# Attention and MLP on one core: query rows of the middle chunk in a tile of their own, small copies on ScalarE, and a second h phase issued ahead over eight banks

## The chip, the core and the metric

The kernel runs on one core of one Trainium2 chip. The metric is the device time of a launch in microseconds (us). A core has TensorE (PE; its weight loads are shown apart as PEld), VectorE (DVE), ScalarE (ACT), GpSimd (POOL) and SyncE (SP). Each runs its own instruction list and waits for the others by semaphores. The kernel's matmuls write to eight PSUM banks of 512 float32 columns.

## What is computed

Eight batches, eight heads of width 64, 512 local and 32 global tokens. Global queries see all 544 keys; a local query sees the 32 global keys and the local keys at most 32 positions away. The result, 4352 tokens of 512 features, goes through an MLP with a quick GELU.

```python
s_g = scale * q_g @ [k_g, k_l].T            # softmax over 544 keys
s_ll = where(|i - j| <= 32, scale * q_l @ k_l.T, -1e9)
s_l = [scale * q_l @ k_g.T, s_ll]           # softmax over 32 + 512 keys
attn = concat(sm(s_g) @ [v_g, v_l], sm(s_l) @ [v_g, v_l])
x = attn as (8*544, 512)
h = x @ w_in                                # 512 -> 2048
out = (h * sigmoid(1.702 * h)) @ w_out      # 2048 -> 512
```

## The kernel before

**Quads.** A batch's eight heads are two quads of four heads, side by side in four groups of 32 partitions. `nq[b]` holds the two quads of batch b; they are called `a` (first) and `c` (second). The 64 features of a token are kept as 32 pairs of bf16, one pair in four bytes, so that one 4-byte 32x32 transpose on VectorE (`Tk` for keys, `Tq` for queries) turns a whole quad. A local token is 16 r + t: its query lies in the tile `qt` at row t + 4, place r (`qt` is 24 rows of 32 four-byte places; rows 0 to 3 and 20 to 23 are filled up with global queries). A matmul takes one half of each pair (`e` is 0 or 1) and so reads every second bf16.

**Attention of a quad of the class `Wide` (batches 2 to 7, 12 quads).** `Tk` and `Tq` turn keys and queries; `ext` (line 530) adds the global queries to `qt` by three VectorE copies (lines 536 to 538) and the global keys to `kT` by a fourth (540). `S(0)` and `S(1)` (line 542) are the scores of two rounds of three parts each, by the table `PARTS` (line 510): six sets of four matmuls per round, one per head, side by side. The middle chunk (c = 2: keys 192 to 319, query places 10 to 21) is part of both rounds: 10 rows of 12 places in round 0, 9 rows of 12 in round 1. Both read `qt[:, row, 10:22]`, 48 bytes out of each row's 128. `X` is the exponential on ScalarE, `M` the mask on VectorE, `U` and `Gm` (lines 569 and 583) the products with values, and `RXG` the normalisation on VectorE, which writes `xL`, the MLP's input.

**Phases.** The order of the work on every engine is the order in which the code issues it (`tc.manual_schedule()`). The h phase of batch i is 16 steps `h_step(i, fc)` (line 617): four matmuls of 512 columns into a PSUM bank (606), tanh on ScalarE (613, tile `th`, two buffers), and a multiply-add on VectorE (614) that writes `gT` and frees the bank. The banks `hp` come from the pool `psP`, which has four; the other four are two pairs of banks, `psS`, given out by `spair()` for the scores. The o phase of batch i (`phase_o`, line 837) is four tiles of 16 matmuls (631), and between them the attention of the next quads: `c` of batch i + 1, then `a` of batch i + 2.

**Around the change.** Batches 0 and 1 use the class `Quad` and an order written out by hand. In batch 0's o phase (lines 769 to 811) the attention of batch 1 is made; `nq[2][0].Tq()` and `transpose_g(4, 6, "k")` (lines 794 and 795) stand behind `a.R()`. Then comes batch 1's h phase (lines 816 to 835): two steps' matmuls issued ahead (818), `G()` of batch 1's second quad behind step 1, `a.Tk()` behind step 2, the turning of global queries and `a.ext()` behind step 7, `a.S(0)` and `a.X(0)` behind step 10, and `a.M(0)` at the end. `phase_o(1)` then begins with `c.T()` and `c.ext()` (849 and 850) on VectorE, and PE does `a.S(1)`, `o(0)`, `c.S(0)`. In later batches `a2.T()` and `a2.ext()` (862 to 864) and `a2.S(0)` lie in the o phase before, and the h phase holds nothing but the 16 steps (890 to 892). `k32` and `q32` (134 and 135) are float32 tiles for the first load, `th4` (737) holds four tanh results of batch 0's h phase.

Of the kernel before, what the change touches and what calls it, by code (L numbers as in the profile page):

```python
# [12 lines left out]
F32 = mybir.dt.float32  # L13
BF16 = mybir.dt.bfloat16
# [6 lines left out]
def kernel(  # L21
# [91 lines left out]
    def load_g(lo, hi, names="kqv"):  # L113
        for name, dst, src in (("k", rkg, kgf), ("q", rqg, qgf)):
            if name in names:
                nc.gpsimd.dma_start(out=dst[:, lo:hi, :], in_=src[:, lo:hi, :])
        if "v" in names:
            load_turned(nc.gpsimd, rvg[:, lo:hi, :D], vgf[:, lo:hi, :])
# [12 lines left out]

    load(0, kq=False)
    rk, rq = loaded[0]
    k32 = ld.tile([128, 16 * D], F32, name="k32", bufs=1)
    q32 = ld.tile([128, 16 * D], F32, name="q32", bufs=1)
    halves = (slice(0, 8 * D), slice(8 * D, 16 * D))
    load_g32("q", qgf)
    for f in halves:
# [95 lines left out]
    def transpose_g(lo, hi, names="qk"):  # L234
        for name, dst, s in (("q", qgT, rqg), ("k", kgT, rkg)):
            if name not in names:
                continue
            nc.vector.transpose(dst[:, lo:hi, :32], s[:, lo:hi].bitcast(F32))
# [37 lines left out]
    def spair():  # L276
        return [psS.tile([128, 2, 512], F32, name="s4", tag="s%d" % i) for i in range(2)]
# [4 lines left out]
    class Quad:  # L282
# [17 lines left out]
        def Tk(self, lo=0, hi=16):  # L300
            if lo == 0:
                self.kT = att.tile([128, Sl], F32, name="kT", bufs=2)
                self.k = self.kT.bitcast(BF16).rearrange("p (m e) -> p m e", e=2)
            nc.vector.transpose(self.kT.rearrange("p (r t) -> p t r", t=16)[:, lo:hi],
                                loaded[self.b][0][:, self.u].bitcast(F32)[:, 32 * lo : 32 * hi])
# [9 lines left out]
        def ext(self, cs=(0, 1, 2, 3)):  # L315
            for c in cs:
                (r0, nr), t0, n = WIN[c], (0, 20, 1, 20)[c], (4, 3, 3, 4)[c]
                nc.vector.tensor_copy(
                    self.qt[:, t0 : t0 + n, r0 : r0 + nr],
                    qgT[:, self.Q, : n * nr].rearrange("p (t r) -> p t r", t=n))  # L320
# [49 lines left out]
        def X(self, rnd, between=None):  # L370
            e = self.E[rnd]
            if len(self.ps) == 4:
                for j in range(4):
                    n = RW + 32 if j == 2 else RW
                    nc.scalar.activation(e[:, j, :n], self.ps[j][:, :n], AF.Exp, scale=scale)
                return
            for i in range(2):
                if i and between:
                    between()
                nc.scalar.activation(e[:, 2 * i : 2 * i + 2, :RW], self.ps[i][:, :, :RW], AF.Exp, scale=scale)  # L380
            if rnd == self.gr:
                nc.scalar.activation(e[:, 2, RW:], bank(self.ps, 2)[:, RW : RW + 32], AF.Exp, scale=scale)
# [136 lines left out]
    OUTER = ((0, 0, 128), (0, 472, 96), (1, 160, 128), (1, 460, 96), (1, 0, 96))  # L519

    class Wide(Quad):
        def Tk(self):
            self.kT = att.tile([128, 4, 320], F32, name="kT", bufs=2)
            flat = self.kT.rearrange("p c s -> p (c s)")
            nc.vector.transpose(flat[:, 0:Sl].rearrange("p (r t) -> p t r", t=16),  # L525
                                loaded[self.b][0][:, self.u].bitcast(F32))
            nc.vector.tensor_copy(self.kT[:, 2:4, 0:96], self.kT[:, 0:2, 96:192])
            self.k = flat.bitcast(BF16).rearrange("p (m e) -> p m e", e=2)

        def ext(self):  # L530
            def g(n, r, m):
                src = qgT[:, self.Q, : n * r].rearrange("p (t o r) -> p t o r", o=1, r=r)
                return src.to_broadcast([128, n, m, r])

            ends = self.qt[:, 0:4, :].rearrange("p t (g r) -> p t g r", r=8)
            nc.vector.tensor_copy(ends[:, :, 0:4:3], g(4, 8, 2))
            nc.vector.tensor_copy(self.qt[:, 20:23, 4:28].rearrange("p t (g r) -> p t g r", r=12), g(3, 12, 2))
            nc.vector.tensor_copy(self.qt[:, 1:4, 10:22],
                                  qgT[:, self.Q, :36].rearrange("p (t r) -> p t r", r=12))
            nc.vector.tensor_copy(self.kT[:, :, 96:128], kgT[:, self.Q : self.Q + 1].to_broadcast([128, 4, 32]))  # L540

        def S(self, rnd):
            self.ps = spair()
            for c, r_, at, lo, hi, _, _, _, r0, nr in PARTS:
                if r_ != rnd:
                    continue
                n = (hi - lo) * nr
                for e in range(2):
                    for j in range(4):
                        p = slice(32 * j, 32 * j + 32)  # L550
                        nc.tensor.matmul(  # L551
                            bank(self.ps, j)[:, at : at + n],
                            lhsT=self.k[p, KEYS[c] : KEYS[c] + 128, e],
                            rhs=self.q[p, lo:hi, r0 : r0 + nr, e],
                            start=(e == 0), stop=(e == 1), skip_group_check=True,
                        )
            self.E[rnd] = att.tile([128, 4, EW], BF16, name="e%d" % rnd)

        def X(self, rnd):
            n = (EW, EW - 12)[rnd]  # L560
            for i in range(2):
                nc.scalar.activation(self.E[rnd][:, 2 * i : 2 * i + 2, :n], self.ps[i][:, :, :n], AF.Exp, scale=scale)  # L562

        def M(self, rnd):
# [39 lines left out]
    def h_mm(i, fc, hp, kcs):  # L604
        for kc in kcs:
            nc.tensor.matmul(hp[:, : width(i)], lhsT=w_in_c[:, fc // 8, kc, fc % 8 // 2, :, fc % 2],  # L606
                             rhs=(xL[i] if i < B else xG)[:, kc, :],
                             start=(kc == 0), stop=(kc == NKC - 1))
# [8 lines left out]
    def h_step(i, fc):  # L617
        if fc == 0:
            gTs[i] = moe.tile([128, FC, TB], BF16, name="gT")
        hp = pbank("hp")  # L620
        h_mm(i, fc, hp, range(NKC))
        h_act(i, fc, hp)
# [111 lines left out]
            h_mm(0, fc, bank(pt, fc), (kc,))  # L734
    a.G()
    c.Gm()
    th4 = th4s[0] = ld.tile([128, 4, TB], F32, name="th4", bufs=1)

    def tanh2(hf):
        f = slice(2 * hf, 2 * hf + 2)  # L740
# [18 lines left out]
    def osteps(i, *sts):  # L759
        for tci, f4 in sts:  # L760
            o_mm(i, 4 * tci + f4)
# [22 lines left out]
    c.S(0)  # L784
    c.X(0)
    c.M(0)
    osteps(0, (2, 2), (2, 3))
    c.S(1)
    a.ekUs(c, 1)
# [1 line left out]
    for unit in range(3):  # L791
        a.U(unit)
    a.R()
    nq[2][0].Tq()
    transpose_g(4, 6, "k")
    c.M(1)
    c.eg()
    pt = spair()
# [14 lines left out]
    load_v(3)  # L813
    load(4)
    load_g(8, NQ, "kq")
    gTs[1] = moe.tile([128, FC, TB], BF16, name="gT")
    hps = [pbank("hp") for _ in range(2)]
    for fc, kcs in ((0, (0, 1)), (1, (0, 1)), (0, (2, 3)), (1, (2, 3))):
        h_mm(1, fc, hps[fc], kcs)
    for fc in range(FC):  # L820
        if fc < 2:
            h_act(1, fc, hps[fc])
        else:
            h_step(1, fc)
        if fc == 1:
            nq[1][1].G()
        if fc == 2:
            a.Tk()
        if fc == 7:
            transpose_g(4, 6, "q")  # L830
            a.ext()
        if fc == 10:
            a.S(0)
            a.X(0)
    a.M(0)

    def phase_o(i):
        b = i + 1
        n = b + 1
        a, c = nq[b]  # L840
        if n < B:
            nq[n] = (Wide(2 * n), Wide(2 * n + 1))
            a2, c2 = nq[n]

        def o(tci):
            for f4 in range(4):
                o_mm(i, 4 * tci + f4)

        c.T()
        c.ext()  # L850
        a.S(1)
        a.X(1)
        a.M(1)
        o(0)
        c.S(0)
        a.UG()
        c.X(0)
        a.RXG()
        c.M(0)
        o(1)  # L860
        if n < B:
            a2.T()
            transpose_g(2 * n, 2 * n + 2)
            a2.ext()
        c.S(1)
        c.X(1)
        c.M(1)
        if n < B:
            o(2)
            a2.S(0)  # L870
            c.UG()
            a2.X(0)
        else:
            for f4 in range(3):
                o_mm(i, 8 + f4)
            for unit in range(3):
                c.U(unit)
            c.Gm(bank(spair(), 0))
            o_mm(i, 11)
        c.RXG()  # L880
        if n < B:
            a2.M(0)
        o(3)
        if i + 3 < B:
            load_v(i + 3)
        if i + 4 < B:
            load(i + 4)

    for i in range(1, B):
        if i > 1:  # L890
            for fc in range(FC):
                h_step(i, fc)
        if i + 1 < B:
            phase_o(i)
    for st in range(FC):
# [35 lines left out]
```

## Time and profile before

| | us |
|---|---|
| Median of 3 runs | 303.5 (302.71 to 303.75) |
| The profiled execution's own time | 303.15 |
| Its span, from first to last instruction | 301.4 |
| PE / DVE / ACT / POOL busy | 292.7 / 218.3 / 167.3 / 75.5 |
| Batch 1's h phase on PE, first to last step | 53.9 to 69.6 |
| First score matmul of batch 2's second quad | 74.89 |
| Batch 2's h phase to the same point | 123.5 to 141.6 |

The profile gives times from the span's start. A group line names the source line, engine, operation, output <- input, shape and count, then the busy time, the mean duration of one in ns, and the idle time of the engine ahead of it with what ended it. A matmul's duration runs from its start to its result, so matmuls overlap: 512-column matmuls last 379 ns and start 216 ns apart. The granted TensorE clock was 1.00 throughout. VectorE and ScalarE instructions also overlap a little; the multiply-adds of line 614 last up to 689 ns and start 604 ns apart when nothing holds them up.

### The profile page before, as it was taken

Reading aid. Unit: us, or ns where it says so; the run is one execution under the profiler, and the core shown is the slowest. Engines: PE = TensorE matmul, PEld = TensorE weight load, DVE = VectorE, ACT = ScalarE, POOL = GpSimd, SP = SyncE. Lnnn points to the kernel's source line nnn. Section 1 sums busy time; section 2 is a strip of 40 time slices with the busy share of each in tenths; the row PEclk is TensorE's granted clock in tenths of the full one; section 3 lists DMA queues with packets and bytes.
Section 4 is the critical chain, followed back from the end, with each engine's and each line's share of the span. In section 5 each row is a group of like instructions: output and inputs, shape, how many; then the busy total and the mean of one; then the engine's idle time right before and its main releaser. Section 6 shows DMA issues by size and latency. Waiting matters only on the chain.

```text
span 301.4 us, 8146 instructions
## 1 busy us (share of the span) xinstructions
PE 292.7 (97%) x3409; PEld 150.1 (50%) x3409; DVE 218.3 (72%) x445; ACT 167.3 (56%) x258; POOL 75.5 (25%) x126
## 2 busy tenths in 40 slices
PE   6899999998999999999999999999999999999995
PEld 6454445443554455445454455445454455446653
DVE  6578857879976887778967887788877866683320
ACT  4838484476537756476446736567447651763421
POOL 8742655972045000900054002600000000000000
PEclk9999999999999999999999999999999999999999
DMA  7999999999459512990269412900220012101122
GB/s 191 178 209 209 206 180 226 123 181 183 66 78 145 100 37 54 124 153 7 70 70 145 86 38 72 124 0 11 63 63 10 0 48 64 35 0 28 44 69 71
DMA packets 59220, 28.35 MB, mean 94 GB/s; under 512 B 47664, under 2 KB 49072, under 8 KB 59184
## 3 DMA queue, kind: packets, MB, share of 16 engines
q0 software_dynamic: 51024, 17.57, 51.9%
q1 hardware_dynamic: 7680, 9.61, 12.0%
q10 hardware_dynamic: 480, 0.66, 0.7%
q8 instruction: 26, 0.43, 0.6%
q14 instruction: 10, 0.08, 0.1%
HBM read 36.31 MB, written 8.91 MB: 150 GB/s over the span
## 4 chain that ended last, share of the span: by engine, by line
PE 84%; DVE 5%; DMA 4%; ACT 4%; issue 1%; SPq 0%; ACTq 0%
PE op L631 35%; PE hp L606 33%; PE ov L577 5%; PE s L551 4%; DVE gT L614 2%; DMA ek<-ek 2%; DMA g32k<-in_k_g_dram 2%; ACT th L613 1%; PE s L606 1%; ACT e L380 1%; PE ov L459 1%; PE op L643 1%; ACT e L562 1%; DVE e L567 1%; DVE kT L525 1%
## 5 line engine op out<-in xcount | busy, mean ns | idle before, releaser
L631 PE MATMUL op<-w_out_sb,gT 128*128 128x512 bf16 x528 | 121.8, 380 | 0.0
L614 DVE SCALAR_TENSOR_TENSOR gT<-th,hp 128x512 bf16<-128x512 f32 (+1 forms) x140 | 91.2, 657 | 41.3 <-ACT th L613 40.2
L606 PE MATMUL hp<-xL,w_in_sb 128*128 128x512 bf16 x496 | 109.2, 379 | 0.5 <-DVE xL L492 0.2
L613 ACT ACTIVATE th<-hp 128x512 f32<-128x512 f32 (+1 forms) x140 | 79.8, 573 | 43.9 <-PE hp L606 39.7
L606 PEld LDWEIGHTS <-w_in_sb 128*128 128x128 bf16 x576 | 56.1, 98 | 65.4 <-issue 1.8
L631 PEld LDWEIGHTS <-gT 128*128 128x128 bf16 x528 | 49.3, 98 | 55.3 <-issue 0.9
L645 ACT ACTIVATE ob<-op 128x512 f32<-128x512 f32 (+2 forms) x35 | 20.5, 585 | 71.8 <-PE op L631 69.3
L97 POOL DMA_DIRECT2D v<-in_v_l_dram x30 | 23.9, 800 | 98.3 <-PE og L588 94.0
L562 ACT ACTIVATE e<-s 128x1016 bf16<-128x1016 f32 (+1 forms) x48 | 45.7, 1005 | 1.2 <-PE s L551 1.0
L567 DVE TENSOR_TENSOR e<-e,mask 128x1760 bf16<-128x1760 bf16 (+1 forms) x24 | 25.0, 1040 | 2.2 <-ACT e L562 2.2
L483 DVE STREAM_TRANSPOSE sT<-ov 128x512 f32<-128x512 f32 x15 | 10.8, 717 | 15.5 <-PE ov L577 11.6
L492 DVE TENSOR_TENSOR xL<-ov,rs 128x512 bf16<-128x512 f32 x30 | 19.3, 686 | 1.5 <-PE ov L459 0.2
L551 PE MATMUL s<-q,kT 32*128 32x160 bf16 (+3 forms) x576 | 16.1, 243 | 0.9 <-DVE kT L540 0.9
L551 PEld LDWEIGHTS <-kT 32*128 32x128 bf16 x576 | 11.1, 94 | 11.3 <-issue 5.1
L380 ACT ACTIVATE e<-s 128x856 bf16<-128x856 f32 x14 | 11.7, 881 | 5.1 <-PE s L347 5.1
L99 POOL DMA_DIRECT2D v<-in_v_g_dram x24 | 13.9, 580 | 2.4 <-DMA rk<-in_k_l_dram 2.1
L525 DVE STREAM_TRANSPOSE kT<-rk 128x512 f32<-128x512 f32 x12 | 12.5, 1041 | 0.0
L487 DVE STREAM_TRANSPOSE rs<-rT 128x512 f32<-128x512 f32 x16 | 11.4, 711 | 0.6
L308 DVE STREAM_TRANSPOSE q<-rq 128x512 f32<-128x512 f32 (+1 forms) x17 | 11.3, 662 | 0.2 <-ACT rq L669 0.2
L577 PE MATMUL ov<-e,v 128*32 128x128 bf16 (+3 forms) x576 | 11.0, 223 | 0.0
L606 PE MATMUL hp<-xG,w_in_sb 128*128 128x256 bf16 x64 | 9.6, 273 | 0.0
L577 PEld LDWEIGHTS <-v 128*32 128x32 bf16 x576 | 9.1, 97 | 0.1
(105 smaller groups left out, 173.8 us busy)
## 6 DMA issues: line engine op xcount, KB each, us to landing
out_dram<-ob SPq DMA_DIRECT2D x132, 64.0 KB, 1.9
rk<-in_k_l_dram POOLq DMA_DIRECT2D x6, 512.0 KB, 9.4
rq<-in_q_l_dram POOLq DMA_DIRECT2D x5, 512.0 KB, 7.5
v<-in_v_l_dram POOLq DMA_DIRECT2D x24, 96.0 KB, 4.5
w_out_sb<-in_moe_w_out_dram POOLq DMA_DIRECT2D x4, 512.0 KB, 10.5
v<-in_v_l_dram POOLq DMA_DIRECT2D x14, 128.0 KB, 6.7
rq<-in_q_l_dram POOLq DMA_DIRECT2D x5, 256.0 KB, 8.9
w_in_sb<-in_moe_w_in_dram POOLq DMA_DIRECT2D x4, 256.0 KB, 6.7
```

Of the source, the lines that this page charges most:

```text
L97: nc.gpsimd.dma_start(out=vt[0:n, :, c, :D], in_=vs[FIRST[c] : FIRST[c] + n])
L492: nc.vector.tensor_mul(self.x[:, 2 * self.u + h, :], self.st[1 + h], self.st["rs"])
L525: nc.vector.transpose(flat[:, 0:Sl].rearrange("p (r t) -> p t r", t=16), loaded[self.b][0][:, self.u].bitcast(F32))
L551: nc.tensor.matmul(bank(self.ps, j)[:, at : at + n], lhsT=self.k[p, KEYS[c] : KEYS[c] + 128, e], rhs=self.q[p, lo:hi, r0 : r0 + nr, e], st ...
L562: nc.scalar.activation(self.E[rnd][:, 2 * i : 2 * i + 2, :n], self.ps[i][:, :, :n], AF.Exp, scale=scale)
L567: nc.vector.tensor_mul(e, e, mask[:, rnd : rnd + 1, :n].to_broadcast([128, 4, n]))
L577: nc.tensor.matmul(ov[32 * j : 32 * j + 32, :].rearrange("p (t r) -> p t r", t=16)[:, t0:t1, r0 : r0 + nr], lhsT=lv, rhs=self.E[rnd][:, j, ...
L606: nc.tensor.matmul(hp[:, : width(i)], lhsT=w_in_c[:, fc // 8, kc, fc % 8 // 2, :, fc % 2], rhs=(xL[i] if i < B else xG)[:, kc, :], start=( ...
L613: nc.scalar.activation(th[:, :n], hp[:, :n], AF.Tanh, scale=0.851)
L614: nc.vector.scalar_tensor_tensor(gTs[i][:, fc, :n], in0=th[:, :n], scalar=1.0, in1=hp[:, :n], op0=ALU.add, op1=ALU.mult)
L631: nc.tensor.matmul(op, lhsT=gTs[i][:, fc, tci * 128 : tci * 128 + 128], rhs=w_out_sb[:, fc, :], start=(first and fc == 4 * f4), stop=(fc = ...
L645: nc.scalar.activation(ob[:, lo:hi], op[:, lo:hi], AF.Copy, scale=0.5)
```

## The change

1. `k32`, `q32` and, later, `th4` share one tile, `early`.
2. Each `Wide` quad gets a tile `qc` of 20 rows of 12 places. `Tq` copies places 10 to 21 of the turned rows into it (a new VectorE copy), `ext` writes the global queries there, and the matmuls of the middle chunk read `qc` in place of `qt`.
3. The copies of `ext` are in parts 0 to 3, move bf16 pairs as bf16 in place of float32, and can be given to ScalarE (`on_act`, an ACTIVATE with Copy).
4. Batch 0's o phase: `nq[2][0].Tq()` and the turning of global keys stand earlier, behind `c.M(0)`.
5. Batch 1's h phase: `a.Tk()` stands ahead of it; steps 2 to 5 get the four banks of a `spair()` and their matmuls are issued ahead with those of steps 0 and 1. Behind step 1 come the global queries' turn, behind step 2 `G()`, behind steps 3 to 6 the four copies of `a.ext` on ScalarE, behind steps 7 to 9 three of `c.ext` on ScalarE; the two halves of `a.X(0)` stand behind steps 10 and 11.
6. `phase_o`: `c.Tk()` only for i = 1; `c.Tq()` and part 3 of `c.ext` remain. In the h phases of batches 2 to 6 `Tk()` of the next second quad stands behind step 4, and parts 0, 1, 2 of its `ext` on ScalarE behind steps 3, 5, 7.

```diff
-    k32 = ld.tile([128, 16 * D], F32, name="k32", bufs=1)
-    q32 = ld.tile([128, 16 * D], F32, name="q32", bufs=1)
+    early = ld.tile([128, 4, TB], F32, name="early", bufs=1)
+    k32, q32 = (early[:, 2 * i : 2 * i + 2].rearrange("p a b -> p (a b)") for i in range(2))
...
     class Wide(Quad):
+        qc = None
+
+        def near_q(self):
+            if self.qc is None:
+                self.qc = att.tile([128, 20, 12], F32, name="qc", bufs=2)
+
+        def Tq(self):
+            Quad.Tq(self)
+            self.near_q()
+            nc.vector.tensor_copy(self.qc[:, 4:20].bitcast(BF16), self.qt[:, 4:20, 10:22].bitcast(BF16))
+
-        def ext(self):
+        def ext(self, parts=range(4), copy=None):
+            copy = copy or nc.vector.tensor_copy
+            qt = self.qt.bitcast(BF16)
+            qg = qgT[:, self.Q, :].bitcast(BF16)
...
+            if 0 in parts:
+                copy(qt[:, 0:4, :].rearrange("p t (g r) -> p t g r", r=16)[:, :, 0:4:3], g(4, 8, 2))
+            if 1 in parts:
+                copy(qt[:, 20:23, 8:56].rearrange("p t (g r) -> p t g r", r=24), g(3, 12, 2))
+            if 2 in parts:
+                self.near_q()
+                copy(self.qc[:, 1:4, :].rearrange("p t r -> p (t r)").bitcast(BF16), qg[:, :72])
+            if 3 in parts:
+                copy(self.kT.bitcast(BF16)[:, :, 192:256],
+                     kgT[:, self.Q : self.Q + 1].bitcast(BF16).to_broadcast([128, 4, 64]))
...
+                qs = self.q[:, lo:hi, r0 : r0 + nr]
+                if c == 2:
+                    qs = self.qc[:, lo:hi].bitcast(BF16).rearrange("p t (r e) -> p t r e", e=2)
...
-                            rhs=self.q[p, lo:hi, r0 : r0 + nr, e],
+                            rhs=qs[p, :, :, e],
...
-    th4 = th4s[0] = ld.tile([128, 4, TB], F32, name="th4", bufs=1)
+    th4 = th4s[0] = early
...
     c.M(0)
+    nq[2][0].Tq()
+    transpose_g(4, 6, "k")
     osteps(0, (2, 2), (2, 3))
...
     a.R()
-    nq[2][0].Tq()
-    transpose_g(4, 6, "k")
...
+    a.Tk()
     gTs[1] = moe.tile([128, FC, TB], BF16, name="gT")
     hps = [pbank("hp") for _ in range(2)]
     for fc, kcs in ((0, (0, 1)), (1, (0, 1)), (0, (2, 3)), (1, (2, 3))):
         h_mm(1, fc, hps[fc], kcs)
+    pt = spair()
+    hps += [bank(pt, j) for j in (2, 3, 0, 1)]
+    for fc in range(2, 6):
+        h_mm(1, fc, hps[fc], range(NKC))
+
+    def on_act(out_, in_):
+        nc.scalar.activation(out_, in_, AF.Copy)
+
     for fc in range(FC):
-        if fc < 2:
+        if fc < 6:
             h_act(1, fc, hps[fc])
         else:
             h_step(1, fc)
         if fc == 1:
+            transpose_g(4, 6, "q")
+        if fc == 2:
             nq[1][1].G()
-        if fc == 2:
-            a.Tk()
-        if fc == 7:
-            transpose_g(4, 6, "q")
-            a.ext()
+        if 3 <= fc <= 6:
+            a.ext((fc - 3,), on_act)
+        if 7 <= fc <= 9:
+            c.ext((fc - 7,), on_act)
         if fc == 10:
             a.S(0)
-            a.X(0)
+            a.X(0, (0,))
+        if fc == 11:
+            a.X(0, (1,))
     a.M(0)
...
-        c.T()
-        c.ext()
+        if i == 1:
+            c.Tk()
+        c.Tq()
+        c.ext((3,))
...
             for fc in range(FC):
                 h_step(i, fc)
+                if i + 1 < B:
+                    if fc == 4:
+                        nq[i + 1][1].Tk()
+                    if fc in (3, 5, 7):
+                        nq[i + 1][1].ext(((3, 5, 7).index(fc),), on_act)
```

More of the change, by code (lines that the diff above doesn't have):

```diff
@@ L528, in Tk @@
             self.k = flat.bitcast(BF16).rearrange("p (m e) -> p m e", e=2)
-        def ext(self):
-            def g(n, r, m):
[L532 to L540, printed above, removed]
+        def near_q(self):
[9 more added lines that the diff above has]
+            qg = qgT[:, self.Q, :].bitcast(BF16)
+            def g(n, r, m):
+                src = qg[:, : 2 * n * r].rearrange("p (t o r) -> p t o r", o=1, r=2 * r)
+                return src.to_broadcast([128, n, m, 2 * r])
+            if 0 in parts:
[8 more added lines that the diff above has]
+                     kgT[:, self.Q : self.Q + 1].bitcast(BF16).to_broadcast([128, 4, 64]))
         def S(self, rnd):
@@ L557, in S, with X @@
             self.E[rnd] = att.tile([128, 4, EW], BF16, name="e%d" % rnd)
-        def X(self, rnd):
+        def X(self, rnd, halves=(0, 1)):
             n = (EW, EW - 12)[rnd]
-            for i in range(2):
+            for i in halves:
                 nc.scalar.activation(self.E[rnd][:, 2 * i : 2 * i + 2, :n], self.ps[i][:, :, :n], AF.Exp, scale=scale)
```

## The prediction

> **What bounds the kernel now.** I read four views: busy time by engine, a table of three equal stretches, the chain of work that ended last, and VectorE's timeline where the chain leaves PE.
>
> ```profile
> PE 292.7 (97%) x3409; PEld 150.1 (50%) x3409; DVE 218.3 (72%) x445; ACT 167.3 (56%) x258; POOL 75.5 (25%) x126
> ```
>
> PE is busy all but 8.7 us. A gain must shorten PE's own work or a place where PE waits. The stretches (start:end, length, then busy us of PE, PEld, DVE, ACT, POOL, clock, DMA, GB/s):
>
> ```profile
> 53.90:74.89 20.99, 19.54 (x129) 8.47 (x129) 17.97 (x41) 14.02 (x22) 14.22 (x26) 1.00 1.36 161
> 90.50:111.49 20.99, 20.99 (x226) 10.31 (x225) 16.30 (x29) 14.56 (x22) 4.31 (x7) 1.00 0.77 99
> ```
>
> The later stretch has no PE idle, and the chain there is PE alone. Batch 1's h phase differs: few matmuls get done in the time, VectorE is busiest, and the chain runs through the multiply-adds, the key turn and the tanhs:
>
> ```profile
> 58.41 0.57 DVE gT L614
> 58.98 0.97 DVE kT L525
> 59.98 0.30 DVE kT L527
> 60.28 0.60 DVE gT L614
> 60.97 0.61 ACT th L613
> ...
> 90.50 13.81 PE hp L606 x64
> ```
>
> How much PE loses: batch 2 goes from its first `hp` matmul to `c.S(0)` in 18.06 us (123.53 to 141.60), without `a.S(0)`, which takes 0.72 here. Batch 1's 20.99 therefore hold 20.99 - 18.78 = 2.2 us of waiting. The matmuls' start times place it: 0.43 for `xL` at steps 0 and 1, 0.28, 0.29 and 0.23 for banks at steps 3, 7 and 15, and 1.0 ahead of `c.S(0)`, whose operands VectorE finishes late:
>
> ```profile
> 70.87 0.69 DVE L614 SCALAR_TENSOR_TENSOR gT<-th,hp 128x512 bf16<-128x512 f32 x1
> 71.47 1.07 DVE L567 TENSOR_TENSOR e<-e,mask 128x1760 bf16<-128x1760 bf16 x1
> 72.46 1.04 DVE L525 STREAM_TRANSPOSE kT<-rk 128x512 f32<-128x512 f32 x1
> 73.53 0.26 DVE L527 COPY kT<-kT 128x192 f32<-128x192 f32 x1
> 73.71 0.70 DVE L308 STREAM_TRANSPOSE q<-rq 128x512 f32<-128x512 f32 x1
> ```
>
> In later phases this queue has no `a.M(0)` (line 567) in it and ends 0.4 us early.
>
> **Edit by edit.** *Turning batch 2's first queries earlier.* VectorE idles 1.31 us ahead of 47.72, waiting for PE. `Tq` (0.70), the new `qc` copy and the small transpose (0.13) fit there. The mask and `xL` of batch 1 move up 0.7 us, until `c.R()` waits for PE instead: `xL` ends near 54.64, and step 0's last matmul wants it at 54.98. The 0.43 is gone. If the `qc` copy took 0.46 the gap would still hold it; without the gap the 0.43 comes back.
>
> *The `qc` copy* (12, VectorE, 384 bf16 each): no row has it. Bounds: 0.09, what 36 elements cost start to start (line 538), and 0.40, one element a cycle as line 540 does (128 in 0.13). I take 0.25, nearest to line 567, which does bf16 at 0.56 ns an element. Later o phases hide it: the mask of the second quad ends at 117.9, PE needs it at 118.8.
>
> *Keys turned ahead of the h phase.* `a.G` (0.68) and `Tk` with its copy (1.30) now precede the first multiply-add: 54.56 + 0.68 + 1.30 = 56.54, against 56.45 before. The keys landed by 50.4, when GpSimd's wait for them ends, so `Tk` waits for nothing new.
>
> *Six steps ahead, eight banks.* Steps 0 to 5 need no multiply-add; steps 6 to 9 take banks of `o_out`, of multiply-adds 0 and 1 and of `c.G`; step 10 is the first to wait for the step four before it. PE is there at 53.90 + 40 x 0.216 = 62.5. Two `th` buffers hold multiply-adds to two in 1.41 us (60.20, 61.60, 63.01 in the timeline), so with `c.G` and the global turn among them number 6 starts near 61.3 and ends at 62.0: 0.5 to spare. The 0.80 of bank waits goes.
>
> *Seven small copies on ScalarE there.* Their VectorE forms go (0.5 us per `ext`). On ScalarE the nearest rows are line 382 (32 elements, 203 ns, the next starts 0.08 later) and line 205 (a bf16 Copy of 160, 494 ns, the next 0.38 later, but its source is gathered element by element). Tanh adds 0.94 ns an element. For 72 to 256 contiguous elements I take 0.12 to 0.30 us, 1.3 in all; at line 205's rate 2.4. Each 1.41 us pair of tanhs leaves ScalarE 0.4 free, so two copies at 0.2 just fit; at 0.35 they push the end 0.4 us. I charge 0.1. [...]
>
> *What is late next.* With PE never waiting, the last `hp` matmul starts at 53.90 + 63 x 0.216 + 0.68 (`a.S(0)`) = 68.16, the last multiply-add 1.04 later (55.40 to 56.45 at step 0) at 69.20. Then the queue above, start to start: 0.60 + 0.99 (mask) + 1.08 (`Tk`) + 0.18 + 0.74 (`Tq`, whose result `qc` needs) + 0.25 (`qc`) + 0.28 (part 3 and the signal) = 4.12. So `c.S(0)` starts at 73.32, with ScalarE's 0.1 at 73.4, against 74.89: **1.5 us gained**. PE would be there at 72.6, so 0.8 us of the same wait stays.
>
> *The middle chunk's layout.* Groups of PE by shape:
>
> ```profile
> L577 PE MATMUL ov<-e,v 128*32 128x128 bf16 x192 | 9.0, 219 | 0.0
> L551 PE MATMUL s<-q,kT 32*128 32x160 bf16 x192 | 7.5, 229 | 0.9 <-DVE kT L540 0.9
> ...
> L577 PE MATMUL ov<-e,v 128*32 128x120 bf16 x96 | 5.4, 215 | 0.0
> ...
> L551 PE MATMUL s<-q,kT 32*128 32x120 bf16 x96 | 3.9, 237 | 0.0
> L551 PE MATMUL s<-q,kT 32*128 32x108 bf16 x96 | 3.7, 230 | 0.0
> ```
>
> The middle chunk's 120 columns take longer than 160 of the first part, and 22 ns longer than 120 contiguous ones of line 577. By start times its sets of four follow each other after 71, 71, 65 and 71 ns, where line 577's follow after 52 at 120 columns and, interpolated to 72 columns' 31, 47 at 108. What differs is where a row lies: 48 bytes from byte 40 touch four 16-byte pieces, those from byte 16 or 64 three, 32 bytes two. That reading fits: at some 1.8 ns a piece, 40 pieces (120 columns) give 72 where 71 is measured, 36 (108) 65 for 65 to 71, 57 (228) 103 for 104 to 109, 40 (160) 72 for 70 to 77. Contiguous, 30 and 27 pieces: 53 and 48. That saves 36 to 40 ns a round. Weight loads set no higher floor: quad 0's 80-column scores follow after 40. Of 24 rounds three lie ahead of or in the remaining wait; 21 x 0.038 = **0.8 us**, all on PE's path. Bounds: 0 (something else sets the pace; fewer pieces exclude a loss) and 0.9 (by durations). [...]
>
> *Second quads' keys in the h phases of batches 2 to 6.* The o phase waits for none of this now, so nothing is gained. The price: `Tk` and its copy (1.30) stand between multiply-adds 4 and 5, which are due 0.863 apart and take 0.604; number 5 is 1.04 late. Its bank is wanted by step 9, 1.02 after its usual end (STT usually ends 2.38 after its step's first matmul, step 9 comes 3.45 after step 5, signal 0.05). That is 0.02 a phase, **0.1 us lost** in five. Bounds: 0 and 0.15 a phase, should the pair take 1.45. The three ScalarE copies (0.2 each) have 0.37 a step.
>
> *The shared tile `early`* adds no instruction; its waits are for transfers landed long before. Nothing.
>
> **Sum.** 1.5 + 0.8 - 0.1 = 2.2 us. The profiled execution's own time 303.15 becomes 300.95, so **301.0**; its span 301.4 becomes 299.2. The median of the runs shown is 303.5, 0.35 above that execution; by it the sum would be 301.3, inside the range.
>
> **Rivals.** *The layout saves nothing* (0.8 stays): 301.8. For it: only start times and durations show the excess, no wait does. Against: the excess follows the pieces touched, in four shapes. Chance 0.14. *ScalarE's copies cost line 205's rate:* VectorE's last multiply-add slips 0.4: 301.4. Its gathered source speaks against it. Chance 0.13. *The lead does not do what it says* (a bank or buffer wait comes back, `c.S(0)` stays near 74.9): 302.5. For it: half a microsecond of spare at step 10. Chance 0.09. *Slower:* the key turn in five h phases. Beyond the 1.02 us allowance every 0.1 us that it holds VectorE longer costs 0.5 in all. The gain of 2.3 is eaten when the pair takes 1.76 us instead of 1.30; at 2.0 us it costs 0.7 a phase and gives 304.4. All twelve key turns of line 525 last 1.04, those beside busy GpSimd too. Chance 0.05. Better than forecast, both parts at their upper bounds, 300.3: 0.04. The forecast itself: 0.55.
>
> **Numbers.** The range leaves out the slower rival and most of the third: 300.1 (upper bounds, and 0.2 of scatter between runs) to 302.4. Runs of this kernel tell 0.3%, 0.9 us, from no change. Below 302.6 lie forecast, first, second and best case and half the third: 0.9, less some doubt about an unseen cost, 0.86; within 0.09; slower 0.05.
>
> **What would show it.** Right: VectorE 435 and ScalarE 280 instructions; middle-chunk matmuls of about 216 and 211 ns; the last multiply-add of batch 1's h phase near 69.3, `c.S(0)` near 73.4 after some 0.8 us of waiting; no bank waits in that phase; later h phases of 13.8 us. Wrong: waits of `hp` for line 614 at step 9 of later phases, ScalarE copies near 0.4 us apart, unchanged 237 and 230 ns.

## The result, and the profile after

The changed kernel takes 301.49 us (median of 6 runs, 301.12 to 302.05) against 303.62 (median of 6), a ratio of 0.9927 with a 95% interval of 0.9906 to 0.9949. Its profiled execution takes 301.57 against 303.15 before, its span is 299.7 against 301.4. Below, tanh n and multiply-add n are those of step n of an h phase.

The busy-time view first, then the same two stretches as before (start:end, length, busy us of PE, PEld, DVE, ACT, POOL, clock, DMA, GB/s). The first one starts at batch 1's first `hp` matmul:

```profile
PE 289.7 (97%) x3368; PEld 150.6 (50%) x3409; DVE 218.6 (73%) x435; ACT 169.5 (57%) x280; POOL 75.7 (25%) x126
...
54.05:75.04 20.99, 19.79 (x167) 9.20 (x168) 18.07 (x34) 15.05 (x30) 14.43 (x26) 1.00 1.30 156
90.50:111.49 20.99, 20.83 (x223) 10.29 (x225) 16.73 (x27) 14.35 (x24) 3.41 (x6) 1.00 0.69 96
```

VectorE and ScalarE hold the 435 and 280 instructions that the forecast named. (PE's records miss 41 matmuls in this trace.) In the same 20.99 us batch 1 now gets 167 matmuls done in place of 129. PE's remaining waits there (in all, times, longest):

```profile
PE s L573 <- DVE kT L558: 0.8, 1, 0.8
...
PE hp L628 <- DVE gT L636: 0.3, 1, 0.3
```

The first is the wait ahead of `c.S(0)`, the second one at step 10 (0.4 by PE's start times, which count more than this view does). VectorE's queue ahead of `c.S(0)` (start, length):

```profile
69.45 1.29 DVE L636 SCALAR_TENSOR_TENSOR gT<-th,hp 128x512 bf16<-128x512 f32 x2
70.65 1.07 DVE L589 TENSOR_TENSOR e<-e,mask 128x1760 bf16<-128x1760 bf16 x1
71.64 1.03 DVE L527 STREAM_TRANSPOSE kT<-rk 128x512 f32<-128x512 f32 x1
72.70 0.26 DVE L529 COPY kT<-kT 128x192 f32<-128x192 f32 x1
72.88 0.70 DVE L308 STREAM_TRANSPOSE q<-rq 128x512 f32<-128x512 f32 x1
73.62 0.26 DVE L539 COPY qc<-q 128x384 bf16<-128x384 bf16 x1
73.79 0.22 DVE L558 COPY kT<-kgT 128x256 bf16<-128x256 bf16 x1
```

The queue behind the last multiply-add (70.05) takes 4.02, but that multiply-add is late: 16.0 after the first `hp` matmul, where the forecast had 15.3. `c.S(0)` starts at 74.07.

Two things vary between profiled executions whatever the edit: the first `hp` matmul of batch 1 comes between 53.4 and 58.3, and from the first matmul of the last output to the end of the span 7.3 or 8.9 us pass (among kernels alike in those parts; the cause was not sought). The profiled execution of the run called paired was a slow one (305.82 us at a granted clock of 0.988), which lost 0.8 us once in `c.S(1)`; without that loss its stretch below would be 237.7. So I compare traces by **the stretch**: from batch 1's first `hp` matmul to the first matmul of the last output. It is 240.20 before and 238.34 after, 1.86 less. Of this 0.97 lies ahead of the first `c.S(0)` (20.99 to 20.02) and 0.89 behind it (a later batch's period, from its first `hp` matmul to that of the next batch, is 33.05 in place of 33.20).

### The profile page after: what moved, and what is told of

The parts are those of the page before. It is cut to its first block, busy times and chain, and to the rows that moved or that the text cites. A ratio compares the mean times of both kernels' runs of the same rounds, so it can differ in the third digit from the quotient of the medians.

```text
span 299.7 us, 8119 instructions
## 1 busy us (share of the span) xinstructions
PE 289.7 (97%) x3368; PEld 150.6 (50%) x3409; DVE 218.6 (73%) x435; ACT 169.5 (57%) x280; POOL 75.7 (25%) x126
## 4 chain that ended last, share of the span: by engine, by line
PE 82%; DVE 5%; DMA 4%; ACT 4%; issue 2%; SPq 0%; ACTq 0%
PE hp L628 33%; PE op L653 33%; PE ov L599 5%; PE s L573 4%; DMA ek<-ek 2%; DVE gT L636 2%; DMA g32k<-in_k_g_dram 2%; ACT th L635 2%; PE s L628 2%; PE ov L459 1%; PE ov L433 1%; PE op L665 1%; DVE e L589 1%; PE s L347 1%; ACT e L584 1%
## 5 line engine op out<-in xcount | busy, mean ns | idle before, releaser
L653 PE MATMUL op<-w_out_sb,gT 128*128 128x512 bf16 x497 | 119.1, 379 | 1.9 <-issue 0.5
L636 DVE SCALAR_TENSOR_TENSOR gT<-th,hp 128x512 bf16<-128x512 f32 (+1 forms) x136 | 87.7, 655 | 35.6 <-ACT th L635 32.7
L628 PE MATMUL hp<-xL,w_in_sb 128*128 128x512 bf16 x472 | 105.0, 379 | 0.7 <-DVE gT L636 0.3
L635 ACT ACTIVATE th<-hp 128x512 f32<-128x512 f32 (+1 forms) x136 | 77.4, 573 | 37.6 <-PE hp L628 29.9
L573 PE MATMUL s<-q,kT 32*128 32x160 bf16 (+1 forms) x384 | 12.6, 246 | 0.8 <-DVE kT L558 0.8
```

Of the source, the lines that this page charges most:

```text
L573: nc.tensor.matmul(bank(self.ps, j)[:, at : at + n], lhsT=self.k[p, KEYS[c] : KEYS[c] + 128, e], rhs=qs[p, :, :, e], start=(e == 0), stop= ...
L635: nc.scalar.activation(th[:, :n], hp[:, :n], AF.Tanh, scale=0.851)
L636: nc.vector.scalar_tensor_tensor(gTs[i][:, fc, :n], in0=th[:, :n], scalar=1.0, in1=hp[:, :n], op0=ALU.add, op1=ALU.mult)
L653: nc.tensor.matmul(op, lhsT=gTs[i][:, fc, tci * 128 : tci * 128 + 128], rhs=w_out_sb[:, fc, :], start=(first and fc == 4 * f4), stop=(fc = ...
```

## Experiments

Ratios are to the kernel before, measured beside each. "To c.S(0)" counts from the first `hp` matmul.

| run | median us | ratio (95%) | stretch | to c.S(0) | period |
|---|---|---|---|---|---|
| before | 303.62 | | 240.20 | 20.99 | 33.20 |
| after | 301.49 | 0.9927 (0.9906-0.9949) | 238.34 | 20.02 | 33.05 |
| layout alone | 305.12 | 1.0018 (0.9989-1.0048) | 241.28 | 21.34 | 33.35 |
| no layout | 302.83 | 0.9960 (0.9934-0.9986) | 238.85 | 19.72 | 33.20 |
| rows aligned | 301.86 | 0.9927 (0.9902-0.9953) | 238.37 | 20.08 | 33.05 |
| rows offset | 302.96 | 0.9964 (0.9937-0.9990) | 239.20 | 20.06 | 33.18 |
| paired | 302.44 | 0.9940 (0.9916-0.9964) | 238.46 | 19.36 | 33.05 |
| copies on VectorE | 301.50 | 0.9937 (0.9915-0.9958) | 238.46 | 20.06 | 33.05 |
| keys in o phase | 303.66 | 0.9995 (0.9976-1.0014) | 239.76 | 20.03 | 33.32 |
| late queries | 303.27 | 1.0001 (0.9979-1.0023) | 239.06 | 20.63 | 33.05 |
| lead of two | 302.17 | 0.9940 (0.9918-0.9962) | 238.53 | 20.22 | 33.05 |
| keys twice | 308.86 | 1.0163 (1.0110-1.0216) | 245.10 | 20.04 | 34.39 |
| o ahead | 301.78 | 0.9905 (0.9867-0.9944) | 238.07 | 21.30 | 33.05 |
| paired, o ahead | 300.66 | 0.9887 (0.9845-0.9930) | 237.37 | 20.67 | 33.05 |

The medians of some runs lie further from the changed kernel's than their stretches do: late queries 1.78 us against 0.72 (and 0.2 ahead of the stretch), no layout 1.34 against 0.51, keys in the o phase 2.17 against 1.42. The rest is not in these stretches, and nothing here explains it. The sizes below are those of the stretches, each from one trace.

### The layout alone, and the change without it

Layout alone: the kernel before, with `qc`, its copy in `Tq`, `S` as changed, and `early`. Without it:

```diff
-            nc.vector.tensor_copy(self.qc[:, 4:20].bitcast(BF16), self.qt[:, 4:20, 10:22].bitcast(BF16))
...
-                if c == 2:
-                    qs = self.qc[:, lo:hi].bitcast(BF16).rearrange("p t (r e) -> p t r e", e=2)
```

Part 2 of `ext` then writes `qt` again.

> The kernel before with the middle chunk's layout alone (the qc tile, its copy, the scores that read it, and the shared tile early that makes room for it); the h phases as before. Theory (the layout is worth what PE's start times show): the sets of four of the middle chunk lose 40 ns in round 0 and 25 in round 1 as in the changed kernel, so 12 x (0.040 + 0.025) = 0.8 us less; the qc copy of batch 2 lengthens VectorE's queue ahead of c.S(0) by 0.18, so the span falls from 301.4 to about 300.8 and the ratio is 0.998. Rival (the layout is free, all of the gain comes from batch 1's h phase): span 301.4 to 301.6, ratio 1.000.

> The changed kernel without the layout: the middle chunk's scores read the old tile again and there is no qc copy. Theory (layout worth 0.8, the h phase 0.9): span 299.7 + 0.8 - 0.2 (the copy's 0.18 goes from the queue ahead of c.S(0)) = 300.3, the middle chunk's matmuls at 237 and 230 ns again, c.S(0) 0.2 earlier. Rival (layout free): span 299.5 and the ratio that of the changed kernel.

Without the layout the stretch behind `c.S(0)` is 0.81 longer (219.13 against 218.32), and `c.S(0)` comes 0.30 earlier since the copy is gone. The layout is worth 0.8 on PE, and its copy costs 0.3 of that in batch 2: 0.18 of its own, and 0.11 because it waits for the end of `Tq` (it starts 0.74 after `Tq` does, the next copy of the kernel before 0.63). The ratio points the same way (0.9960 against 0.9927), though the two intervals overlap. Alone, the layout shortened the middle chunk's matmuls just as much (212 ns both) and still lost 1.1 in the stretch: neither theory. Of this 0.35 lies ahead of `c.S(0)`, and the period grew by 0.15. VectorE of the kernel before, ahead of `a.U` of batch 3, shows how much room there was:

```profile
105.58 1.04 DVE L525 STREAM_TRANSPOSE kT<-rk 128x512 f32<-128x512 f32 x1
...
106.83 0.70 DVE L308 STREAM_TRANSPOSE q<-rq 128x512 f32<-128x512 f32 x1
...
107.87 1.04 DVE L567 TENSOR_TENSOR e<-e,mask 128x1712 bf16<-128x1712 bf16 x1
```

`a.M(1)`, the last row, ends at 108.91; PE starts `a.U` at 109.01. From the key turn's start to the mask's start 2.29 us pass here, and 2.60 with the layout alone: there is no room for a copy that delays the mask by 0.3. PE of the run with the layout alone (`a.U`'s first part is the `ones` row; it took 0.55 before):

```profile
110.00 0.70 PE L590 MATMUL ov<-e,ones 128*32 128x128 bf16 x24
110.51 1.04 PE L590 MATMUL ov<-e,v 128*32 128x128 bf16 x48
111.36 0.35 PE L601 MATMUL og<-v,e 128*32 128x66 bf16 x20
```

From `a.U` to `a.Gm` 1.36 us pass in place of 1.10. This made the run with the keys in the o phase, below, worth making.

### What it is in the layout

```diff
-                self.qc = att.tile([128, 20, 12], F32, name="qc", bufs=2)
+                self.qc = att.tile([128, 20, 16], F32, name="qc", bufs=2)[:, :, 0:12]
```

The offset form has `[:, :, 2:14]`.

> The changed kernel with the rows of qc 64 bytes apart, each row's 48 bytes from byte 0: no unbroken run any more, but still three 16-byte pieces a row (30 and 27 pieces a set, as in the unbroken tile). Theory A (the sets cost by 16-byte pieces): from the first set of four of the middle chunk to what follows the second, 212 ns in round 0 and 111 in round 1 as in the changed kernel; span 299.7. Theory B (an unbroken run is what is cheap): 252 and 136 ns as before the change; span 300.5. Theory C (the tile's layout costs nothing and the durations mislead): span 299.7 whatever the start times.

> As the run with aligned rows 64 bytes apart, but each row's 48 bytes from byte 8, so that it touches four 16-byte pieces (40 and 36 a set, as in the old tile). Theory A (cost by pieces): 252 and 136 ns again for the middle chunk's two sets in rounds 0 and 1, span 299.7 + 0.8 = 300.5. Theory B (unbroken run): also 252 and 136. If A is right the two runs differ by 0.8 us, if B they are equal and both at 300.5; if both stay at 212 and 111 the gain came from neither but from reading a tile of its own.

The groups of PE by shape, busy us and mean ns of one, first of the changed kernel with its unbroken tile:

```profile
L573 PE MATMUL s<-qc,kT 32*128 32x120 bf16 x96 | 3.4, 212 | 0.0
L573 PE MATMUL s<-qc,kT 32*128 32x108 bf16 x96 | 3.3, 212 | 0.0
```

Then of the run with aligned rows:

```profile
L573 PE MATMUL s<-qc,kT 32*128 32x108 bf16 x96 | 3.3, 212 | 0.0
L573 PE MATMUL s<-qc,kT 32*128 32x120 bf16 x96 | 3.3, 210 | 0.0
```

And with offset rows:

```profile
L573 PE MATMUL s<-qc,kT 32*128 32x120 bf16 x96 | 3.8, 232 | 0.0
L573 PE MATMUL s<-qc,kT 32*128 32x108 bf16 x96 | 3.7, 228 | 0.0
```

By start times, from the first set of the middle chunk to what follows the second, 204 ns (round 0) and 111 ns (round 1) pass with aligned rows, 212 and 111 in the unbroken tile, 244 and 133 with offset rows, 252 and 136 in the old tile. The same 48 bytes in rows 64 bytes apart are fast or slow by where they begin, and the stretch differs by 0.83. Theory B falls, since an unbroken run is not needed, and so does theory C. Theory A holds in these four layouts: the cost goes with the 16-byte pieces touched. Both slow layouts begin their rows 8 bytes past a multiple of 16, so a price for each row that begins there would fit as well; no run tells the two apart.

### The pair of banks

ScalarE and then VectorE of the changed kernel through steps 2 to 5 (in brackets, idle time ahead and what ended it):

```profile
57.70 0.60 ACT L635 ACTIVATE th<-s 128x512 f32<-128x512 f32 x1 [1.07 <-PE s L628]
59.05 0.60 ACT L635 ACTIVATE th<-s 128x512 f32<-128x512 f32 x1 [0.75 <-DVE gT L636]
...
61.08 0.60 ACT L635 ACTIVATE th<-s 128x512 f32<-128x512 f32 x1 [0.54 <-DVE gT L636]
```

```profile
58.33 0.69 DVE L636 SCALAR_TENSOR_TENSOR gT<-th,s 128x512 bf16<-128x512 f32 x1 [0.25 <-ACT th L635]
...
59.68 1.37 DVE L636 SCALAR_TENSOR_TENSOR gT<-th,s 128x512 bf16<-128x512 f32 x2
61.71 0.69 DVE L636 SCALAR_TENSOR_TENSOR gT<-th,s 128x512 bf16<-128x512 f32 x1 [0.66 <-ACT th L635]
```

Tanh 2 waits until step 3's matmuls are done too: step 2's last one ended at 56.80, step 3's at 57.66, and it starts at 57.70. Tanh 3 starts at 59.05, 0.03 after multiply-add 2 ends; its matmuls and its `th` buffer had been ready since 57.92. Tanh 5 starts 0.03 after multiply-add 4. The view names multiply-adds as what ended both waits. Each had read the other bank of the same pair: a pair of banks is one tile, and the reading is that its readers on two engines are put in order though they read different banks. Where two steps' banks are in different tiles, tanh and multiply-add run side by side: tanh 6 on `hp` from 61.73 to 62.32, multiply-add 5 on the pair from 61.71 to 62.40.

```diff
-        if fc < 6:
+        if fc < 2:
             h_act(1, fc, hps[fc])
+        elif fc in (2, 4):
+            pr, th2 = pt[(4 - fc) // 2], early[:, fc - 2 : fc]
+            nc.scalar.activation(th2, pr, AF.Tanh, scale=0.851)
+            nc.vector.scalar_tensor_tensor(gTs[1][:, fc : fc + 2, :], in0=th2, scalar=1.0, in1=pr,
+                                           op0=ALU.add, op1=ALU.mult)
+        elif fc < 6:
+            pass
```

> The changed kernel, with steps 2 and 3 of batch 1's h phase, and 4 and 5, each taken by one tanh and one multiply-add of 1024 columns over the pair of banks that they share. Theory (the two-bank tile is the cause: the tanh of one step waits for the matmuls of both and for the multiply-add of the other, so multiply-adds 3 to 6 come 0.4 to 1.0 late): no such wait is left, multiply-add 6 starts near 61.6 in place of 62.35 (first hp matmul at 54.05), the 0.4 wait of PE at step 10 goes, the last multiply-add comes 15.4 after the first hp matmul (16.0 in the changed kernel) and c.S(0) 19.4 (20.0): span 299.7 - 0.6 = 299.1. Rival (ScalarE's seven copies and two th buffers set the pace): last multiply-add and c.S(0) within 0.2 of 16.0 and 20.0, span 299.7.

The last multiply-add comes at 15.33 and `c.S(0)` at 19.36, as the theory said, and the wait at step 10 is gone. ScalarE, in this run:

```profile
61.92 1.02 ACT L856 ACTIVATE early<-s 128x1024 f32<-128x1024 f32 x1 [1.07 <-PE s L628]
63.64 1.02 ACT L856 ACTIVATE early<-s 128x1024 f32<-128x1024 f32 x1 [0.51 <-PE s L628]
```

Both paired tanhs wait for their matmuls alone. The median does not separate this run from the changed kernel; the last run below holds the same edit and gives the same 15.33. Fewer instructions account for little: the two paired multiply-adds hold VectorE 1.14 and 1.11 us where two single ones hold it 1.21. The edit also takes these steps off the two `th` buffers. In the changed kernel those buffers did not hold tanhs 2 to 5 up: each came free 0.4 to 1.1 us ahead of the tanh that took it.

```diff
-    pt = spair()
-    hps += [bank(pt, j) for j in (2, 3, 0, 1)]
-    for fc in range(2, 6):
-        h_mm(1, fc, hps[fc], range(NKC))
...
-        if fc < 6:
+        if fc < 2:
```

> The changed kernel with a lead of two steps in batch 1's h phase, as before, and its banks from the pool of four (steps 2 to 5 no longer in the two pairs); the rest of the change stays. The forecast's reading (step b: the lead of six took away 0.8 of bank waits): these waits are back and c.S(0) comes 20.8 after the first hp matmul (20.0 in the changed kernel), span 300.5. Rival, from the wait of each tanh for its pair (the lead costs what it gives; the multiply-adds at 0.70 a step need a bank only every 0.58): some bank waits are back, tanhs 2 to 6 come as early as PE and VectorE allow, c.S(0) at 19.5 to 20.0, span 299.2 to 299.7.

One bank wait returned, at step 3 for multiply-add 0 (0.9 by PE's start times; the view of waits has it shorter):

```profile
PE hp L628 <- DVE gT L636: 0.7, 1, 0.7
```

The last multiply-add came at 16.20 and `c.S(0)` at 20.22: between the two, nearer to the rival, though its span was missed (300.6; this execution began 0.7 later). So the lead of six as written gives 0.2, and with the pairs taken together 0.87 (16.20 to 15.33), about the 0.80 of bank waits that the forecast counted.

### The copies on ScalarE, and the early queries

```diff
-            a.ext((fc - 3,), on_act)
+            a.ext((fc - 3,))
...
-            c.ext((fc - 7,), on_act)
+            c.ext((fc - 7,))
```

> The changed kernel with the seven small copies of batch 1's h phase on VectorE. Theory (their place is worth little: on ScalarE they take 1.4 us, of which the multiply-adds from step 7 on feel 0.07 each; on VectorE they take 0.8 us, most of it in the hole of 0.66 between multiply-adds 4 and 5): c.S(0) 19.9 to 20.2 after the first hp matmul (20.0), span 299.6 to 299.9. Rival (the copies on ScalarE are what kept the forecast's other 0.5 us): c.S(0) at 19.5, span 299.2.

No difference (20.06 against 20.02): this rival falls. On ScalarE the copies last 0.25 to 0.42 us, and the tanh that follows starts 0.15 or 0.19 after one of 72 elements and 0.20 after one of 128.

```diff
-    nq[2][0].Tq()
-    transpose_g(4, 6, "k")
     osteps(0, (2, 2), (2, 3))
...
     a.R()
+    nq[2][0].Tq()
+    transpose_g(4, 6, "k")
```

> The changed kernel with batch 2's first queries turned where they were before, behind a.R(). Theory (the move took away the wait for xL at steps 0 and 1): PE waits 0.4 for xL again, tanh 1 and with it the multiply-adds are 0.4 late, c.S(0) 0.3 to 0.5 later after the first hp matmul (20.0) or the h phase starts 0.2 to 0.5 later: span 300.1 to 300.3. Rival (the multiply-adds from step 2 on set the end, so the start has room): span 299.7.

The wait for `xL` is back, and the last multiply-add and `c.S(0)` come 0.6 later; ahead of the phase another 0.2 goes (6.93 from `a.U` to the first `hp` matmul, 6.71 in the changed kernel). Theory, with a larger size: 0.9 in all. The run with the layout alone shows where most of the excess over the forecast's 0.43 comes from. It has the old order and the `qc` copy, and there too 6.94 pass from `a.U` and PE waits 0.53 for `xL`, in place of 6.71 and 0.43 in the kernel before: the copy in that place of the queue costs 0.3.

### The second quads' keys

Keys in the o phase:

```diff
-        if i == 1:
-            c.Tk()
+        c.Tk()
         c.Tq()
-        c.ext((3,))
+        c.ext((3,) if i == 1 else range(4))
...
-                    if fc == 4:
-                        nq[i + 1][1].Tk()
-                    if fc in (3, 5, 7):
-                        nq[i + 1][1].ext(((3, 5, 7).index(fc),), on_act)
```

> The changed kernel with the second quads' keys turned and their small copies made in the o phase again, ahead of a.M(1), for batches 3 to 7; batch 2 as in the changed kernel. The prediction's theory (the o phase waits for none of this, moving it gains nothing): span 299.7 or 0.1 less, period of a later batch 33.05. Rival, from the run with the layout alone (there the qc copy, behind the key turn, made a.M(1) end 0.27 after PE's first a.U matmul, and a.U to a.Gm took 1.36 in place of 1.10): the move is what hides the qc copy, 0.25 us in each of five batches, period 33.3, span 300.9.

Period 33.32, stretch 1.42 longer: the rival. `a.M(1)` of batch 3 in this run:

```profile
108.08 1.04 DVE L589 TENSOR_TENSOR e<-e,mask 128x1712 bf16<-128x1712 bf16 x1
```

It ends at 109.12, when PE has been at `a.U` since 108.82. In the changed kernel it ends at 106.94, 1.06 ahead of `a.U`, which starts at 108.00:

```profile
105.89 1.05 DVE L589 TENSOR_TENSOR e<-e,mask 128x1712 bf16<-128x1712 bf16 x1
```

Keys turned twice in the h phases:

```diff
                     if fc == 4:
                         nq[i + 1][1].Tk()
+                        nq[i + 1][1].Tk(True)
```

(`Tk(True)` turns into the same `kT` once more.)

> The changed kernel with the key turn and its copy made twice in the five later h phases (the same result written twice). The prediction's price for the slower rival (all that exceeds an allowance of 1.02 us is lost in each of five phases): the pair takes 1.25 in the changed kernel, twice that is 2.50, multiply-add 5 comes 2.25 late, 1.23 a phase is lost at step 9, 6.1 us in all: span 305.8, period 34.3 in place of 33.05. Rival (the phase has more slack than the allowance, since only the bank of multiply-add 5 is late and PE has eight steps to make it good): 0 to 2 us, span 299.7 to 301.7.

PE's waits for multiply-adds, of which five are in these phases:

```profile
PE hp L629 <- DVE gT L637: 6.1, 6, 1.2
```

The period is 34.39: 1.34 a phase lost where 1.23 was worked out, 6.8 in the stretch. The phase has an allowance and no more slack than that.

### A version that beats both

```diff
-        if i == 1:
-            c.Tk()
-        c.Tq()
-        c.ext((3,))
+        if i > 1:
+            c.Tq()
+            c.ext((3,))
         a.S(1)
         a.X(1)
         a.M(1)
         o(0)
+        if i == 1:
+            c.Tk()
+            c.Tq()
+            c.ext((3,))
+            a.UG()
         c.S(0)
-        a.UG()
+        if i > 1:
+            a.UG()
```

> The changed kernel, with batch 2's a.UG ahead of c.S(0) and c.Tk, c.Tq and c.ext behind a.M(1), in that batch alone. Theory (between 54 and 86 us VectorE's queue sets the pace, and PE's waits of 0.9 ahead of c.S(0) and 0.3 in a.UG are where it shows): PE runs a.UG behind o(0) with no wait, c.S(0) waits some 0.6 us and starts 21.2 after the first hp matmul, c.S(1) at 25.4 (25.8 in the changed kernel), span 299.3. Rival (VectorE is late at a.RXG just as much and c.UG pays it back): span 299.7.

> Both the paired steps 2 to 5 and a.UG ahead of c.S(0). If the two-bank tile cost 0.6 us by making VectorE's queue late, the queue behind the last multiply-add comes 0.6 earlier, c.S(0) at 20.6 to 20.7 after the first hp matmul, c.S(1) at 24.8 to 24.9, the wait at step 10 is gone: span 298.7, 0.6 less than with a.UG ahead alone. If the pairing only moves a wait, this run and the one with a.UG ahead alone give the same.

With `a.UG` ahead, `c.S(1)` comes 25.47 after the first `hp` matmul, near the theory's 25.4, and the stretch falls by 0.27 (the span of this execution holds the longer end and a start 1.8 later). The median, 301.78 of 14 runs, does not show it. With both, `c.S(1)` comes at 24.84 and the stretch is 237.37, 0.70 less than with `a.UG` ahead alone: the pairing's gain is kept to the end. The median is 300.66, ratio 0.9887, the lowest of all; its interval overlaps that of the changed kernel, so that it beats this one rests on the traces. The chain that ended last, for this run (start, length, work): it goes through PE from step 2 to step 15, where the chain before went through multiply-adds and tanhs.

```profile
56.26 3.45 PE s L628 x16
59.71 4.32 PE hp L628 x20
64.03 0.57 PE s L573 x20
64.60 4.44 PE hp L628 x20
```

## Why the prediction came out as it did

The forecast of 301.0 is 0.5 below the median and 0.6 below the profiled execution; the stretch gained 1.86 of the forecast's 2.2. The medians gained 2.13, but the six runs before spread over 2.2 us, so that this comes so near is partly luck. The direction held, and so did the layout's term of 0.8; the first term, 1.5, came out at 0.97.

- **The wait for `xL`**: gone, as forecast. Its value was put at 0.43; undoing the move costs 0.9, because the `qc` copy then stands in the same queue without cover (0.3 by the run with the layout alone). The forecast named that condition, but charged nothing beyond the 0.43 for it.
- **Six steps ahead, eight banks**: this step failed. "Step 10 is the first to wait" was right, but "0.5 to spare" was not: step 10 waited 0.4. The forecast counted eight banks as eight buffers. Four of them are two tiles, and each tanh on a tile waited for both its steps' matmuls or for the other step's multiply-add. That made the last multiply-add 0.7 late. Less 0.1 that the queue behind it gained and 0.1 charged to ScalarE's copies that did not come, it is the miss in `c.S(0)` (20.0 against 19.5). Paired instructions brought 15.33, the forecast's 15.3.
- **ScalarE's copies**: 0.15 to 0.20 to what follows a copy of 72 or 128 elements, inside the 0.12 to 0.30 taken; their place is worth nothing that shows. A copy of 128 lasted 0.30 to 0.32, and the tanh behind it started 0.20 after its start. The 0.94 ns an element taken for the tanh is near the 0.48 to 0.50 us that a tanh of 512 columns of the kernel before took from its start to the next; by durations, 598 ns at 512 columns and 383 at 256, an element added 0.84.
- **The queue behind the last multiply-add**: 4.02 for 4.12; the `qc` copy took 0.18 for 0.25. Its upper bound of 0.40 is three times line 540's 0.13 for 128 elements; no run shows the cycle it is put down to.
- **The middle chunk's layout**: 0.8 forecast, 0.81 measured, and the reason given (pieces touched) fits all four layouts. It gives the sum of a round better than each set: the rounds lost 40 and 35 ns, as forecast, but single sets came out at 60, 62 and 49 ns where 53 and 48 were worked out, and the first set of round 1 hardly moved (65 to 62). Of the four set times that the prediction reads from the kernel before, the last set of round 0 has none in the trace, since other work follows it, after 181 ns. The rival that it saves nothing is refuted by the run without it.
- **Keys of second quads**: "the o phase waits for none of this now, so nothing is gained" failed as a description of the changed kernel. The forecast checked cover for the `qc` copy at the second quad's mask only. At the first quad's, `a.M(1)`, the kernel before had no room, and this move gives the room: 1.4 us over five batches. Both parts were in the change, so the sum did not suffer. The loss charged (0.1) did not come: the phases take 13.91 from their first `hp` matmul to `a.S(1)` in both kernels. The price given for the slower rival, all that exceeds the allowance, held within 0.11 a phase.

## What to carry over

Eight banks were not eight buffers here, because the waits went by tile and a tile held two of them: where two steps share a tile, take them in one instruction, as the run called paired did, or give each its own, which was not tried with eight. When a change adds work to an engine's queue, look for the consumer with the least room behind each place of that queue, not for the nearest one; two parts that look independent can be one part and its cover. Compare executions over a stretch that leaves out the start and the end if those vary by more than the effect.

## What the runs showed of the hardware

In the four layouts tried, the time of scores whose moving operand lies in rows of 48 bytes went with the 16-byte pieces touched: sets of four of 120 columns in 30 pieces followed each other after 57 to 60 ns, in 40 pieces after 69 to 71; in unbroken bf16 columns of line 577 it was 52. A matmul of 120 columns in 40 pieces lasted 232 to 237 ns, in 30 pieces 210 to 212. The bf16 copy of 384 elements on VectorE lasted 0.26 us, and the next instruction started 0.18 after its start.
